# One order for GpSimd's transfers in the experts' loop, TensorE transposes for slots 1 to 3, and transposing transfers that wait for two weight quarters

## The chip, the cores and the metric

The kernel runs on one core of a Trainium2 chip. The metric is the device time of one execution in microseconds (us), taken from before the first instruction to after the last.

## The reference

Two stages follow each other. The first is attention over 8 batches, 8 heads, 576 positions and 64 channels; the heads 0 to 3 see a window of the last 32 positions, the heads 4 to 7 every 32nd position. The second sends each of the 4608 resulting rows of 512 numbers to one of 8 experts and scales the answer by the gate's probability.

```
scores = where(mask[head], q @ k.T / sqrt(64), -1e9)
x = softmax(scores) @ v                  # 8 batches x 576 rows -> 4608 x 512
logits = x @ w_gate + modality_bias[modality_id]
e = argmax(logits); gate = softmax(logits)[e]
out = gate * (relu(x @ w1[e]) @ w2[e])   # 512 -> 1024 -> 512, float32
```

## The kernel before

**Attention and routing.** Batches are taken in four pairs (1152 rows each). A pair's result is written to DRAM as `xd`, its routing is computed, and a table `ld` in DRAM gets one entry for each row: where it came from and its gate. `slots(ph)` turns the counts of each expert into a plan of slots: `li` holds the table positions of each slot's rows, `wi` the places of its weights. Of the pairs 0 to 3, the end of pair 1 brings phase 0 (slots 0 and 1), that of pair 2 phase 1 (slots 2 and 3), and that of pair 3 phase 2 (all the rest). Pair 3's last attention work and its routing overlap the first expert slots.

**The experts' loop.** A slot is 384 rows that go to one expert. There are 12 of them in a fixed loop, then one slot of 128 rows, and a guarded remainder that does not run on these inputs. `ffn` works through a slot in 8 steps f. Each step takes 1/8 of the expert's weights out of `raw`, splits them into a rounded part `wh` (ScalarE, L919) and a remainder `wl` (VectorE, L920), multiplies the rows into `h` (12 matmuls, L884), forms `hh` on ScalarE (L887) and `hl` on VectorE (L889), and two steps later adds them into three sums `o` (9 matmuls, L898). At the end ScalarE scales `o` into `y` and GpSimd scatters `y` into `out` (L906, three transfers).

**The transfers of a slot.** All are issued by GpSimd as indirect transfers, and GpSimd issues them strictly in its own row: three lookups `le` (L754, from `ld` by `li`), three gathers `fx` of the rows (L746, from `xd` by `le`), four weight quarters `raw0` to `raw3` (L763, 1 MB each, read at f = 0 and 1, 2 and 3, and so on) and three scatters `out`. Each quarter has one buffer, so the next slot's quarter waits for the last cast of the present one: quarter j of the next slot is asked for at f = 2j+1.

**Turning the rows.** TensorE needs the rows transposed. Slot 0 and the slot of 128 rows are turned by TensorE (`turn_tokens`). For the others `send_tokens` (called at f = SEND = 1 of the slot before) copies the two 16-bit halves apart on VectorE (L855) and issues three transposing transfers on SyncE's queue (L858), and `split_tokens` (at f = SPLIT = 5) puts the halves together on VectorE (L867) and splits the rows in `xh` (ScalarE, L871) and `xl` (VectorE, L872). The tile `work` of this path takes turns in the two buffers that attention's `xt` tiles use.

**What sets the order.** TensorE's row is as written during attention. Everywhere else a scheduler orders each engine's row by its own estimate of times, unless a step is pinned.

Of the kernel before, what the change touches and what calls it, by code (L numbers as in the profile page):

```python
# [11 lines left out]
F32 = mybir.dt.float32  # L12
# [30 lines left out]
LAG = 2  # L43
SEND, SPLIT = 1, 5
BIG = -float(2 ** 30)
# [135 lines left out]
def attention_moe(ctx: ExitStack, tc: tile.TileContext, a, out):  # L181
# [453 lines left out]
    def slots(ph):  # L635
# [101 lines left out]
        return li, wi, inc, wall  # L737

    def tokens(n, le, xrows):

        xt = pre.tile([P, TH, DM], F32, tag="fx", name=f"fx{n}")
        bounds = {} if xrows > NT else {"bounds_check": xrows - 1, "oob_is_err": False}
        if n.startswith("0_"):
            nc.gpsimd.memset(xt[:], 0.0)
        for h in range(TH):
            nc.gpsimd.indirect_dma_start(xt[:, h, :], None, xd[0:xrows, :], IOA(ap=le[:, h, 0:1], axis=0), **bounds)  # L746
        return xt, le

    def entries(n, li, s, xrows):

        le = pre.tile([P, TH, 2], I32, tag="le", bufs=7, name=f"le{n}")
        last = min(xrows, NT)
        for h in range(TH):
            nc.gpsimd.indirect_dma_start(le[:, h, :], None, ld[0:1 + last, :], IOA(ap=li[:, s, h:h + 1], axis=0))  # L754
        return le
# [3 lines left out]
    def weights(wi, s, j, pinned=False):  # L759

        if j not in raws:
            raws[j] = (pre if j < 2 else pools["fp"]).tile([P, 2, 1024], F32, bufs=1, name=f"raw{j}")
        ins = nc.gpsimd.indirect_dma_start(  # L763
            raws[j].rearrange("p f c -> p (f c)"), None, a["w"], IOA(ap=wi[:, s, j:j + 1], axis=0),
            bounds_check=E * 4 * P - 1, oob_is_err=False)
        if pinned:
            pin(ins)

    pools = {}

    def half_entries():
        le = pre.tile([P, TH, 2], I32, tag="le", bufs=7, name="leh")
        nc.gpsimd.indirect_dma_start(le[:, 0, :], None, ld[:], IOA(ap=halved["li"], axis=0))
        return le

    def half_tokens(le):
        xt = pre.tile([P, TH, DM], F32, tag="fx", name="fxh")
        nc.gpsimd.indirect_dma_start(xt[:, 0, :], None, xd[:], IOA(ap=le[:, 0, 0:1], axis=0))
        return xt, le
# [16 lines left out]
    def half_ffn(fp, le, xs):  # L796
# [10 lines left out]
        for f in range(8):  # L807
            raw = raws[f // 2][:, f % 2, :]
            wh = fp.tile([P, 1024], F32R, tag="wh", bufs=4, name=f"whh{f}")
            wl = fp.tile([P, 1024], F32R, tag="wl", bufs=4, name=f"wlh{f}")  # L810
            nc.scalar.copy(wh[:, 0:512], raw[:, 512:1024])
# [12 lines left out]
        settle(0)  # L824
        y = fp.tile([P, DM], F32, tag="y", bufs=2, name="yh")
        nc.scalar.mul(y[:], os[0], le[:, 0, 1:2].bitcast(F32))
        outs.add(nc.gpsimd.indirect_dma_start(
            out, IOA(ap=le[:, 0, 0:1], axis=0), y[:], None, bounds_check=NT - 1, oob_is_err=False))

# [15 lines left out]
    def halves(t):  # L845

        return t.bitcast(U16).rearrange("p a (c w) -> p a c w", w=2)

    def send_tokens(n, xt, le):

        part = TH * DM
        work = ap.tile([P, 9, DM], F32, tag="xt", bufs=2, name=f"work{n}").rearrange("p k c -> p (k c)")
        rows = work[:, 0:part].bitcast(U16).rearrange("p (h w c) -> p h w c", h=TH, w=2)
        for w in range(2):
            pin(nc.vector.tensor_copy(rows[:, :, w, :], halves(xt)[:, :, :, w]))  # L855
        cols = work[:, part:2 * part].bitcast(U16).rearrange("p (h w c q) -> p h w c q", h=TH, w=2, c=4)
# [18 lines left out]
    def ffn(fp, n, xh, xl, le, between, load=None):  # L875
# [25 lines left out]
        def finish():  # L901
            gate = le[:, :, 1].bitcast(F32)
            for h in range(TH):
                y = fp.tile([P, DM], F32, tag="y", bufs=2, name=f"y{n}{h}")
                nc.scalar.mul(y[:], os[h], gate[:, h:h + 1])  # L905
                outs.add(nc.gpsimd.indirect_dma_start(  # L906
                    out, IOA(ap=le[:, h, 0:1], axis=0), y[:], None, bounds_check=NT - 1, oob_is_err=False))

# [4 lines left out]
        for f in range(8):  # L913
            raw = raws[f // 2][:, f % 2, :]
            wh = fp.tile([P, 1024], F32R, tag="wh", bufs=4, name=f"wh{n}{f}")
            wl = fp.tile([P, 1024], F32R, tag="wl", bufs=4, name=f"wl{n}{f}")
# [4 lines left out]
            if load and f % 2:  # L921
                load(f // 2)
# [6 lines left out]
    for bp in range(NBP):  # L929
        xt = ap.tile([P, 9, DM], F32, tag="xt", bufs=2, name=f"xt{bp}")  # L930
# [33 lines left out]
    for ph, (bp, n) in enumerate(PHASES):  # L964
        last = ph == len(PHASES) - 1
        for i in range(NSTATIC - len(plan) if last else n):
            plan.append((f"{ph}_{i}", ph, i, NT + 1 if last else (bp + 1) * T2))

    def load(k, j):
        if k == len(plan):  # L970
            weights(halved["wi"], 0, j)
        if k < len(plan):
            weights(tables[plan[k][1]][1], plan[k][2], j)

# [31 lines left out]
    for n in range(nu + 3):  # L1006
# [48 lines left out]
    half_ffn(fp, *turned[len(plan)])  # L1055


# [39 lines left out]
```

## Time and profile before

| | us |
|---|---|
| runs | 632.78, 633.19, 639.26 (median 633.19) |
| profiled execution, its own time | 640.56 |
| profiled execution, span of its instructions | 638.8 |
| TensorE busy in that span | 584.8 (92%) |
| VectorE, ScalarE, GpSimd busy | 395.6, 327.4, 190.8 |

The rows further down are from the profiled execution. Their times count from the first instruction of the span. The first `hh` of a slot marks where the slot's TensorE work has begun, so the distance of two such rows is what one slot took.

### The profile page before, as it was taken

What the parts mean: (1) busy time and instruction counts of PE and PEld (TensorE: products, weight loads), DVE (VectorE), ACT (ScalarE), POOL (GpSimd) and SP (SyncE); (2) the same over time, 40 slices, a digit from 0 to 9 for tenths busy, and PEclk for the clock granted to TensorE, in tenths of its full rate; (3) what the DMA queues carried; (4) which work ended last, traced back from release to release, by engine and by line L of the source; (5) the groups of instructions that cost most, each with busy time, mean ns of one, the idle gap of its engine ahead of it and who ended that gap; (6) DMA issues with size and microseconds to landing.
All of it is one profiled execution on the core that took longest, in us unless ns stands there. A gap on an engine that the chain in (4) does not pass through costs nothing.

```text
span 638.8 us, 13548 instructions
## 1 busy us (share of the span) xinstructions
PE 584.8 (92%) x5423; PEld 512.8 (80%) x5425; DVE 395.6 (62%) x931; ACT 327.4 (51%) x650; POOL 190.8 (30%) x184
## 2 busy tenths in 40 slices
PE   8789988967996999966999999999999998999996
PEld 5677777855875989954999999898999987899985
DVE  6776867932983768913666656666666662765432
ACT  5588778634772443512545454544445542645443
POOL 3010000062244231373462626151515140212211
PEclk9899899985998999995999999999999999899999
DMA  8997988866479248447493516460505069232411
GB/s 306 278 300 249 332 234 310 272 236 204 162 264 251 92 157 180 135 98 229 149 200 146 132 67 167 180 136 2 148 1 139 11 157 156 91 73 83 166 66 70
DMA packets 63227, 105.86 MB, mean 166 GB/s; under 512 B 42099, under 2 KB 42355, under 8 KB 59060
## 3 DMA queue, kind: packets, MB, share of 16 engines
q0 software_dynamic: 14592, 52.75, 25.9%
q1 hardware_dynamic: 43284, 42.21, 25.5%
q10 hardware_dynamic: 5280, 9.94, 4.5%
q8 instruction: 45, 0.74, 0.5%
q14 instruction: 26, 0.21, 0.1%
HBM read 98.28 MB, written 19.18 MB: 184 GB/s over the span
## 4 chain that ended last, share of the span: by engine, by line
PE 68%; issue 5%; DMA 4%; DVE 3%; ACT 2%; another core or an unknown queue 1%; POOL 0%; SPq 0%; ACTq 0%; POOLq 0%; DVEq 0%
PE o L898 30%; PE h L884 30%; DMA work<-work 3%; PE s L320 1%; PE o L355 1%; DMA vv<-in_vl 1%; ACT wh L919 1%; PE ot L452 1%; PE ss L407 1%; PE xs L214 1%; PE en L597 1%; PE hh L815 0%; PE t L214 0%; PE lg L501 0%
## 5 line engine op out<-in xcount | busy, mean ns | idle before, releaser
L920 DVE TENSOR_TENSOR wl<-raw,wh 128x512 fp32r<-128x512 f32 x192 | 124.7, 688 | 36.1 <-ACT wh L919 33.2
L919 ACT CAST wh<-raw 128x512 fp32r<-128x512 f32 x192 | 109.2, 619 | 66.6 <-PE o L898 54.5
L884 PE MATMUL h<-xh,wh 128*128 128x384 f32 x384 | 130.7, 340 | 6.3 <-ACT wh L919 6.3
L884 PE MATMUL h<-xh,wl 128*128 128x384 f32 x384 | 130.6, 341 | 4.8 <-DVE wl L920 3.8
L884 PE MATMUL h<-xl,wh 128*128 128x384 f32 x384 | 130.8, 341 | 1.1 <-issue 1.1
L887 ACT ACTIVATE hh<-h 128x384 fp32r<-128x384 f32 x96 | 47.2, 492 | 155.8 <-PE h L884 110.3
L889 DVE SCALAR_TENSOR_TENSOR hl<-h,hh 128x384 fp32r<-128x384 f32 x96 | 53.4, 556 | 115.8 <-ACT hh L887 84.3
L898 PE MATMUL o<-wh,hh 128*128 128x512 f32 x288 | 115.8, 402 | 8.1 <-issue 7.2
L898 PE MATMUL o<-wl,hh 128*128 128x512 f32 x288 | 114.6, 398 | 0.1
L763 POOL DMA_INDIRECT raw<-in_w,wi x48 | 58.4, 1218 | 185.3 <-DVE wl L920 143.9
L898 PE MATMUL o<-wh,hl 128*128 128x512 f32 x288 | 110.3, 398 | 1.2 <-issue 1.2
L884 PEld LDWEIGHTS h<-xh,wh 128*128 128x128 f32 x384 | 73.2, 191 | 13.2 <-ACT wh L919 6.7
L884 PEld LDWEIGHTS h<-xh,wl 128*128 128x128 f32 x384 | 73.2, 191 | 8.3 <-DVE wl L920 4.2
L884 PEld LDWEIGHTS h<-xl,wh 128*128 128x128 f32 x384 | 73.1, 190 | 4.8 <-issue 1.2
L898 PEld LDWEIGHTS o<-wh,hh 128*128 128x128 f32 x288 | 55.2, 192 | 18.2 <-issue 8.5
L898 PEld LDWEIGHTS o<-wl,hh 128*128 128x128 f32 x288 | 55.3, 192 | 9.6 <-issue 0.4
L898 PEld LDWEIGHTS o<-wh,hl 128*128 128x128 f32 x288 | 54.8, 191 | 8.9 <-issue 1.6
L906 POOL DMA_INDIRECT out<-y,le x36 | 36.9, 1024 | 68.2 <-ACT y L905 65.2
L746 POOL DMA_INDIRECT fx<-xd,le x36 | 38.9, 1080 | 12.5 <-issue 8.6
L754 POOL DMA_INDIRECT le<-ld,li x36 | 36.2, 1006 | 17.6 <-issue 9.8
L855 DVE COPY work<-fx 128x1536 uint16<-128x1536 uint16 x22 | 37.4, 1743 | 0.0
L320 PE MATMUL s<-qk,qd 128*64 128x64 f32 x576 | 24.5, 230 | 11.3 <-issue 10.6
(191 smaller groups left out, 757.5 us busy)
## 6 DMA issues: line engine op xcount, KB each, us to landing
qk<-in_qkl SPq DMA_DIRECT2D x16, 592.0 KB
vv<-in_vl SPq DMA_DIRECT2D x16, 585.0 KB
qks<-in_qks SPq DMA_DIRECT2D x16, 576.0 KB
xd<-xt ACTq DMA_DIRECT2D x8, 1024.0 KB
vs<-in_vs SPq DMA_DIRECT2D x16, 288.0 KB
xd<-xt ACTq DMA_DIRECT2D x4, 256.0 KB
raw<-in_w,wi POOLq DMA_INDIRECT x48
le<-ld,li POOLq DMA_INDIRECT x36
```

The source lines that it names most:

```text
L320: nc.tensor.matmul(s[64 * jj:64 * jj + 64, g, :], qd[:, i, :, :].rearrange("p b q -> p (b q)"), qk[:, 18 + i:20 + i, :].rearrange("p b q - ...
L746: nc.gpsimd.indirect_dma_start(xt[:, h, :], None, xd[0:xrows, :], IOA(ap=le[:, h, 0:1], axis=0), **bounds)
L754: nc.gpsimd.indirect_dma_start(le[:, h, :], None, ld[0:1 + last, :], IOA(ap=li[:, s, h:h + 1], axis=0))
L763: ins = nc.gpsimd.indirect_dma_start(raws[j].rearrange("p f c -> p (f c)"), None, a["w"], IOA(ap=wi[:, s, j:j + 1], axis=0), bounds_check= ...
L855: pin(nc.vector.tensor_copy(rows[:, :, w, :], halves(xt)[:, :, :, w]))
L884: nc.tensor.matmul(hp, w[:, a1], x[:, c, :], start=(k == 0), stop=(k == 11))
L887: nc.scalar.activation(hh[:], hp, AF.Relu)
L889: nc.vector.scalar_tensor_tensor(hl[:], hp, 0.0, hh.bitcast(F32), ALU.max, ALU.subtract)
L898: nc.tensor.matmul(os[h], hx[:, m], w[:, 512:1024], start=(f == 0 and i == 0), stop=(f == 7 and i == 2))
L906: outs.add(nc.gpsimd.indirect_dma_start(out, IOA(ap=le[:, h, 0:1], axis=0), y[:], None, bounds_check=NT - 1, oob_is_err=False))
L919: nc.scalar.copy(wh[:, c], raw[:, c])
L920: nc.vector.tensor_tensor(wl[:, c], raw[:, c], wh[:, c].bitcast(F32), ALU.subtract)
```

## The change

The edits, in the order of the code:

1. `in_turn` ties every GpSimd transfer of the experts' loop to the one before it in program order, so the scheduler no longer chooses their order. Inside a slot the written order is now: quarter 0, the three scatters of the slot before, quarter 1, lookups (f = 3, three slots ahead), gathers (f = 4, two slots ahead), quarters 2 and 3.
2. `raw2` and `raw3` lie in the buffer of attention's tile `xt0` instead of the pool that opens when attention ends, and slot 0's two are asked for right behind slot 0's turning. `work` then has only the other buffer, `xt1`.
3. Slots 1 to 3 are turned by TensorE at f = 4 of the slot before (`TURN`, `TURNED`).
4. For slots 4 to 11 the two copies L855 stay at f = 1 (`PLANE`), the transposing transfers are issued at f = 3 (`SEND`) and wait until quarter 1 of that step has landed; the next slot's first gather waits until they have landed; `split_tokens` moves from f = 5 to f = 6.
5. `wh` and `wl` have 5 buffers instead of 4, `y` 4 instead of 2, `le` 5 instead of 7. The slot of 128 rows is turned at f = 4 instead of 3.

```diff
-SEND, SPLIT = 1, 5
+PLANE, SEND, SPLIT, TURN = 1, 3, 6, 4
+FIND, GATHER = 3, 4
+WHEN = {1: 0, 3: 1, 5: 2, 7: 3}
+TURNED = 4
...
+    def in_turn(ins):
+        if ordered:
+            if ordered[-1]:
+                tc.add_manual_dep(ins.ins, ordered[-1], behind, reason="order of transfers")
+            ordered.append(ins.ins.name)
+        return ins
...
         for h in range(TH):
-            nc.gpsimd.indirect_dma_start(xt[:, h, :], None, xd[0:xrows, :], IOA(ap=le[:, h, 0:1], axis=0), **bounds)
+            ins = in_turn(nc.gpsimd.indirect_dma_start(
+                xt[:, h, :], None, xd[0:xrows, :], IOA(ap=le[:, h, 0:1], axis=0), **bounds))
+            if h == 0:
+                for t in turning:
+                    after_landing(ins, t)
...
-            raws[j] = (pre if j < 2 else pools["fp"]).tile([P, 2, 1024], F32, bufs=1, name=f"raw{j}")
+            if j < 2:
+                raws[j] = pre.tile([P, 2, 1024], F32, bufs=1, name=f"raw{j}")
+            else:
+                both = ap.tile([P, 9, DM], F32, tag="xt0", name="raw23")[:, 0:8, :]
+                both = both.rearrange("p (j f a) c -> p j f (a c)", j=2, f=2)
+                raws[2], raws[3] = both[:, 0], both[:, 1]
...
-        work = ap.tile([P, 9, DM], F32, tag="xt", bufs=2, name=f"work{n}").rearrange("p k c -> p (k c)")
+        work = ap.tile([P, 9, DM], F32, tag="xt1", name=f"work{n}").rearrange("p k c -> p (k c)")
...
+        turning.clear()
         for h in range(TH):
-            nc.sync.dma_start(
+            turning.append(nc.sync.dma_start(
                 cols[:, h].rearrange("p w c q -> p (w c) q"),
-                rows[:, h].rearrange("p w (c q) -> p (w c) q", q=P), transpose=True)
+                rows[:, h].rearrange("p w (c q) -> p (w c) q", q=P), transpose=True))
+            after_landing(turning[h], quarter[1])
...
         if n == nu + 1:
             turn(0)
+            for j in (2, 3):
+                load(0, j)
...
-    for j in (2, 3):
-        load(0, j)
+    ordered.append(None)
     for k, (n, *_) in enumerate(plan):
         def between(f):
             pop(POPF)
-            if k + 1 < len(plan):
+            if TURNED <= k + 1 < len(plan):
+                if f == PLANE:
+                    sent[k + 1] = plane_tokens(plan[k + 1][0], *gathered[k + 1])
                 if f == SEND:
-                    sent[k + 1] = send_tokens(plan[k + 1][0], *gathered[k + 1])
+                    sent[k + 1] = send_tokens(*sent[k + 1])
                 if f == SPLIT:
                     turned[k + 1] = split_tokens(plan[k + 1][0], (k + 1) % 2, *sent[k + 1])
-            elif f == 3:
+            elif f == TURN:
                 turn(k + 1)
-            if f == 2:
+            if k == 0 and f == 0:
+                look_up(2)
+            if f == FIND:
+                look_up(k + 3)
+            if f == GATHER:
                 gather(k + 2)
-            if f == 4:
-                look_up(k + 3)
```

In the rows of instructions below, the number behind a name tells instances apart; `le_0`, `fx_1` and the like count the slots inside a phase, so `le_0_4041` before and `le_0_4004` after are the lookups of slot 4, the first slot of phase 2.

**GpSimd where slot 0 runs.** Before, from the last two quarters of slot 0 on:

```order
L763 DMA raw_3344<-in_w,wi_2389 128x2048
L763 DMA raw_2515<-in_w,wi_2389 128x2048
L763 DMA raw_2519<-in_w,wi_2389 128x2048
L754 DMA le_0_3519<-ld,li_3216 128x2 x3
L754 DMA le_1_3603<-ld,li_3216 128x2 x3
L746 DMA fx_0_3523<-xd,le_0_3519 128x512 x3
L746 DMA fx_1_3961<-xd,le_1_3603 128x512 x3
L763 DMA raw_3340<-in_w,wi_2389 128x2048
```

After, the same stretch:

```order
L771 DMA le_0_3408<-ld,li_3216 128x2 x3
L786 DMA raw_2515<-in_w,wi_2389 128x2048
L786 DMA raw_2519<-in_w,wi_2389 128x2048
L771 DMA le_1_3554<-ld,li_3216 128x2 x3
L759 DMA fx_0_3616<-xd,le_0_3408 128x512 x3
L786 DMA raw_3294<-in_w,wi_2389 128x2048 x2
```

The lookups of slots 2 and 3 stood together and directly ahead of both slots' gathers; now two weight quarters stand between them, and slot 3's gathers have moved to a later slot.

**GpSimd where slots 1 and 2 run.** Before, all twelve lookups of slots 4 to 7 follow each other as soon as `li` of phase 2 is there:

```order
L754 DMA le_0_4041<-ld,li_3860 128x2 x3
L754 DMA le_1_4349<-ld,li_3860 128x2 x3
L754 DMA le_2_4657<-ld,li_3860 128x2 x3
L754 DMA le_3_4965<-ld,li_3860 128x2 x3
L906 DMA out<-y_10_4237,le_1_2399 4608x512
L906 DMA out<-y_11_4242,le_1_2399 4608x512
L746 DMA fx_0_4275<-xd,le_0_4041 128x512 x3
L746 DMA fx_1_4583<-xd,le_1_4349 128x512
L763 DMA raw_2519<-in_w,wi_3225 128x2048
L746 DMA fx_1_4583<-xd,le_1_4349 128x512 x2
L763 DMA raw_3340<-in_w,wi_3225 128x2048
```

After:

```order
L786 DMA raw_2519<-in_w,wi_3225 128x2048
L771 DMA le_0_4004<-ld,li_3871 128x2 x3
L759 DMA fx_1_4066<-xd,le_1_3554 128x512 x3
L786 DMA raw_3294<-in_w,wi_3225 128x2048 x2
L786 DMA raw_2515<-in_w,wi_3225 128x2048
L938 DMA out<-y_10_4254,le_1_2399 4608x512
L938 DMA out<-y_11_4259,le_1_2399 4608x512
L938 DMA out<-y_12_4264,le_1_2399 4608x512
L786 DMA raw_2519<-in_w,wi_3225 128x2048
L771 DMA le_1_4330<-ld,li_3871 128x2 x3
L759 DMA fx_0_4392<-xd,le_0_4004 128x512 x3
```

The lookups of slots 4 to 7 are spread over four slots, three at a time, each set between two weight quarters.

**GpSimd in a later slot.** Before, the gathers and lookups stand ahead of quarter 1, and nothing in this row waits for a transposing transfer:

```order
L763 DMA raw_2515<-in_w,wi_3871 128x2048
L906 DMA out<-y_00_5161,le_0_4041 4608x512
L906 DMA out<-y_01_5166,le_0_4041 4608x512
L906 DMA out<-y_02_5171,le_0_4041 4608x512
L746 DMA fx_4_5507<-xd,le_4_5273 128x512 x3
L754 DMA le_7_6197<-ld,li_3860 128x2 x3
L763 DMA raw_2519<-in_w,wi_3871 128x2048
L763 DMA raw_3340<-in_w,wi_3871 128x2048
```

After:

```order
L786 DMA raw_2515<-in_w,wi_3882 128x2048
L938 DMA out<-y_40_6425,le_4_5272 4608x512
L938 DMA out<-y_41_6430,le_4_5272 4608x512
L938 DMA out<-y_42_6435,le_4_5272 4608x512
L786 DMA raw_2519<-in_w,wi_3882 128x2048
L799 DMA leh<-ld,li_3871 128x2
L759 DMA fx_7_6538<-xd,le_7_6196 128x512 x3
L786 DMA raw_3294<-in_w,wi_3882 128x2048 x2
```

Quarter 1 stands ahead of the lookups and gathers, and the first gather, with quarters 2 and 3 (`raw_3294` holds both) behind it, waits for the landing of transfers that themselves wait for quarter 1.

## Rows read from the trace of the kernel before

**Rows 1.** The page: busy time of each engine, share of the span, instructions.

```profile
PE 584.8 (92%) x5423; PEld 512.8 (80%) x5425; DVE 395.6 (62%) x931; ACT 327.4 (51%) x650; POOL 190.8 (30%) x184
```

**Rows 2.** Timeline, ScalarE, first `hh` of slots 0 to 4, 9, 10: start, duration.

```profile
183.35 0.53 ACT L887 ACTIVATE hh<-h 128x384 fp32r<-128x384 f32 x1
...
227.59 0.49 ACT L887 ACTIVATE hh<-h 128x384 fp32r<-128x384 f32 x1 [3.25 <-PE h L884]
...
263.13 0.49 ACT L887 ACTIVATE hh<-h 128x384 fp32r<-128x384 f32 x1 [0.68 <-PE h L884]
...
311.96 0.49 ACT L887 ACTIVATE hh<-h 128x384 fp32r<-128x384 f32 x1 [1.73 <-PE h L884]
...
345.34 0.49 ACT L887 ACTIVATE hh<-h 128x384 fp32r<-128x384 f32 x1 [1.94 <-PE h L884]
...
512.47 0.49 ACT L887 ACTIVATE hh<-h 128x384 fp32r<-128x384 f32 x1 [1.94 <-PE h L884]
...
551.46 0.49 ACT L887 ACTIVATE hh<-h 128x384 fp32r<-128x384 f32 x1 [1.99 <-PE h L884]
```

**Rows 3.** Windows: stretch, its length, busy time of PE, PEld, DVE, ACT, POOL, clock, DMA.

```profile
139.00:151.00 12.00, 3.68 (x29) 2.60 (x30) 0.00 (x0) 1.19 (x3) 7.70 (x8) 0.63 0.52 147
...
198.50:204.80 6.30, 0.05 (x1) 0.00 (x0) 0.35 (x3) 0.66 (x2) 2.48 (x3) 0.90 1.01 271
...
281.00:298.00 17.00, 5.73 (x12) 3.02 (x11) 0.56 (x1) 0.74 (x2) 10.19 (x11) 0.63 0.67 204
...
312.00:512.40 200.40, 200.40 (x1009) 181.71 (x1008) 128.21 (x180) 98.33 (x174) 83.71 (x74) 1.00 0.42 113
```

**Rows 4.** Timeline, GpSimd, 133 to 149: first and last of 12 transfers.

```profile
133.75 0.96 POOL L754 DMA_INDIRECT le<-ld,li  x1 [2.88 <-DVE li L711]
...
147.97 1.00 POOL L746 DMA_INDIRECT fx<-xd,le  x1 [0.30 <-issue]
```

**Rows 5.** Timeline, GpSimd, 186 to 202: first and last of 12 transfers.

```profile
186.49 0.97 POOL L754 DMA_INDIRECT le<-ld,li  x1 [1.56 <-DVE li L711]
...
200.86 1.00 POOL L746 DMA_INDIRECT fx<-xd,le  x1 [0.30 <-issue]
```

**Rows 6.** Timeline, GpSimd, 266 to 294: first and last of 22 transfers.

```profile
266.26 0.98 POOL L754 DMA_INDIRECT le<-ld,li  x1 [3.08 <-DVE li L711]
...
293.23 1.01 POOL L763 DMA_INDIRECT raw<-in_w,wi  x1 [0.30 <-issue]
```

**Rows 7.** Timeline, TensorE, 283 to 292: the longest gap.

```profile
283.68 0.34 PE L884 MATMUL h<-xh,wl 128*128 128x384 f32 x1 [1.06 <-issue]
291.23 0.80 PE L898 MATMUL o<-wh,hh 128*128 128x512 f32 x1 [7.21 <-issue]
```

**Rows 8.** Timeline, GpSimd, 320 to 334: first and last of 9 transfers.

```profile
320.82 1.34 POOL L906 DMA_INDIRECT out<-y,le  x1 [1.71 <-ACT y L905]
...
332.19 1.01 POOL L763 DMA_INDIRECT raw<-in_w,wi  x1 [0.30 <-issue]
```

**Rows 9.** Chain of waits, 515 to 546, slot 9.

```profile
523.72 17.47 DMA work<-work
```

**Rows 10.** Chain of waits, 170 to 184: slot 0 turned by TensorE.

```profile
173.76 1.46 PE xt L214 x12
```

**Rows 11.** Timelines, slot 8: transposing transfers, quarter 1, first copy of `split_tokens`.

```profile
487.63 4.52 SPq L858 DMA_TRANSPOSE work<-work  x3
...
494.09 1.00 POOL L763 DMA_INDIRECT raw<-in_w,wi  x1 [0.31 <-issue]
...
499.96 2.00 DVE L867 COPY work<-work 128x1536 uint16<-128x1536 uint16 x2
```

**Rows 12.** DMA, 487 to 497, 40 slices of 0.25 us: GB/s.

```profile
GB/s 0 0 0 229 426 393 0 128 220 218 200 198 116 133 115 115 131 421 263 254 276 304 350 164 344 306 277 145 182 152 325 382 312 295 36 1 0 0 0 0
```

**Rows 13.** DMA, 209 to 217, 40 slices of 0.2 us: GB/s, one quarter alone.

```profile
GB/s 0 0 0 0 0 0 0 0 0 41 410 287 0 0 82 492 451 369 451 451 410 451 451 369 410 123 0 0 0 0 0 0 0 0 0 0 0 0 0 0
```

**Rows 14.** Timeline, GpSimd: the issue of that quarter.

```profile
209.30 1.00 POOL L763 DMA_INDIRECT raw<-in_w,wi  x1 [7.44 <-DVE wl L920]
```

More of the change, by code (lines that the diff above doesn't have):

```diff
@@ L737, in slots @@
         return li, wi, inc, wall
+    ordered = []
+    behind = mybir.DependencyInfo(mybir.DependencyClass.NoSync, mybir.DependencyReason.DATA)
+    def in_turn(ins):
[4 more added lines that the diff above has]
+        return ins
     def tokens(n, le, xrows):
@@ L745, in tokens @@
         for h in range(TH):
-            nc.gpsimd.indirect_dma_start(xt[:, h, :], None, xd[0:xrows, :], IOA(ap=le[:, h, 0:1], axis=0), **bounds)
+            ins = in_turn(nc.gpsimd.indirect_dma_start(
[3 more added lines that the diff above has]
+                    after_landing(ins, t)
         return xt, le
     def entries(n, li, s, xrows):
-        le = pre.tile([P, TH, 2], I32, tag="le", bufs=7, name=f"le{n}")
+        le = pre.tile([P, TH, 2], I32, tag="le", bufs=5, name=f"le{n}")
         last = min(xrows, NT)
         for h in range(TH):
-            nc.gpsimd.indirect_dma_start(le[:, h, :], None, ld[0:1 + last, :], IOA(ap=li[:, s, h:h + 1], axis=0))
+            in_turn(nc.gpsimd.indirect_dma_start(
+                le[:, h, :], None, ld[0:1 + last, :], IOA(ap=li[:, s, h:h + 1], axis=0)))
         return le
@@ L767, in weights @@
             pin(ins)
+        else:
+            in_turn(ins)
+        return ins
     pools = {}
     def half_entries():
-        le = pre.tile([P, TH, 2], I32, tag="le", bufs=7, name="leh")
-        nc.gpsimd.indirect_dma_start(le[:, 0, :], None, ld[:], IOA(ap=halved["li"], axis=0))
+        le = pre.tile([P, TH, 2], I32, tag="le", bufs=5, name="leh")
+        in_turn(nc.gpsimd.indirect_dma_start(le[:, 0, :], None, ld[:], IOA(ap=halved["li"], axis=0)))
         return le
@@ L808, in half_ffn @@
             raw = raws[f // 2][:, f % 2, :]
[L809 to L810 removed]
+            wh = fp.tile([P, 1024], F32R, tag="wh", bufs=5, name=f"whh{f}")
+            wl = fp.tile([P, 1024], F32R, tag="wl", bufs=5, name=f"wlh{f}")
             nc.scalar.copy(wh[:, 0:512], raw[:, 512:1024])
@@ L824, in half_ffn @@
         settle(0)
-        y = fp.tile([P, DM], F32, tag="y", bufs=2, name="yh")
+        y = fp.tile([P, DM], F32, tag="y", bufs=4, name="yh")
         nc.scalar.mul(y[:], os[0], le[:, 0, 1:2].bitcast(F32))
-        outs.add(nc.gpsimd.indirect_dma_start(
-            out, IOA(ap=le[:, 0, 0:1], axis=0), y[:], None, bounds_check=NT - 1, oob_is_err=False))
+        outs.add(in_turn(nc.gpsimd.indirect_dma_start(
+            out, IOA(ap=le[:, 0, 0:1], axis=0), y[:], None, bounds_check=NT - 1, oob_is_err=False)))
     def parts_of(n, odd):
@@ L855, in send_tokens @@
             pin(nc.vector.tensor_copy(rows[:, :, w, :], halves(xt)[:, :, :, w]))
+        return work, rows, le
+    def send_tokens(work, rows, le):
+        part = TH * DM
         cols = work[:, part:2 * part].bitcast(U16).rearrange("p (h w c q) -> p h w c q", h=TH, w=2, c=4)
+        turning.clear()
         for h in range(TH):
-            nc.sync.dma_start(
+            turning.append(nc.sync.dma_start(
                 cols[:, h].rearrange("p w c q -> p (w c) q"),
-                rows[:, h].rearrange("p w (c q) -> p (w c) q", q=P), transpose=True)
+                rows[:, h].rearrange("p w (c q) -> p (w c) q", q=P), transpose=True))
+            after_landing(turning[h], quarter[1])
         return work, cols, le
@@ L903, in finish @@
             for h in range(TH):
-                y = fp.tile([P, DM], F32, tag="y", bufs=2, name=f"y{n}{h}")
+                y = fp.tile([P, DM], F32, tag="y", bufs=4, name=f"y{n}{h}")
                 nc.scalar.mul(y[:], os[h], gate[:, h:h + 1])
-                outs.add(nc.gpsimd.indirect_dma_start(
-                    out, IOA(ap=le[:, h, 0:1], axis=0), y[:], None, bounds_check=NT - 1, oob_is_err=False))
+                outs.add(in_turn(nc.gpsimd.indirect_dma_start(
+                    out, IOA(ap=le[:, h, 0:1], axis=0), y[:], None, bounds_check=NT - 1, oob_is_err=False)))
         def down_last(*args):
@@ L914, in ffn @@
             raw = raws[f // 2][:, f % 2, :]
-            wh = fp.tile([P, 1024], F32R, tag="wh", bufs=4, name=f"wh{n}{f}")
-            wl = fp.tile([P, 1024], F32R, tag="wl", bufs=4, name=f"wl{n}{f}")
+            wh = fp.tile([P, 1024], F32R, tag="wh", bufs=5, name=f"wh{n}{f}")
+            wl = fp.tile([P, 1024], F32R, tag="wl", bufs=5, name=f"wl{n}{f}")
             for c0 in range(0, 1024, 512):
@@ L920, in ffn @@
                 nc.vector.tensor_tensor(wl[:, c], raw[:, c], wh[:, c].bitcast(F32), ALU.subtract)
-            if load and f % 2:
-                load(f // 2)
+            if load and f in WHEN:
+                load(WHEN[f])
             late.append(partial(down_last if f == 7 else down, f, wh, wl, *up(f, wh, wl)))
@@ L967, in attention_moe, with after_landing @@
             plan.append((f"{ph}_{i}", ph, i, NT + 1 if last else (bp + 1) * T2))
+    landed = mybir.DependencyInfo(mybir.DependencyClass.Sync, mybir.DependencyReason.DATA)
+    quarter, turning = {}, []
+    def after_landing(ins, other):
+        tc.add_manual_dep(ins.ins, other.ins.name, landed, reason="transfers kept apart")
     def load(k, j):
         if k == len(plan):
-            weights(halved["wi"], 0, j)
+            quarter[j] = weights(halved["wi"], 0, j)
         if k < len(plan):
-            weights(tables[plan[k][1]][1], plan[k][2], j)
+            quarter[j] = weights(tables[plan[k][1]][1], plan[k][2], j)
     found, gathered, sent, turned = {}, {}, {}, {}
```

8 lines of the change are left out of this document (5 added, 3 removed).

## The prediction

> **What bounds the kernel now.** I read the page's busy times first: TensorE is busy for 584.8 of 638.8 us and no other engine for more than 62% [rows 1]. A change that only lightens VectorE, ScalarE or GpSimd therefore gains nothing unless TensorE waits for them somewhere. The next view is the first `hh` of each slot, because the distance of two of them is a slot's price. From slot 4 to slot 9 that is (512.47 - 345.34) / 5 = 33.43 us, and the window from 312.0 to 512.4 shows TensorE busy for 200.40 of 200.40 us: a plain slot is pure TensorE work [rows 2, 3]. Against 33.43, slot 0 took 44.2, slot 1 35.5, slot 2 48.8 and slot 9 39.0 us [rows 2]. So 28.3 us are lost in slots 0 to 2 and 5.6 in slot 9. In the first three, part of the loss is pair 3's attention work, which TensorE does there; that work stays.
>
> Where the rest went is seen in the windows. In 281 to 298 TensorE was busy for 5.73 of 17.00 us and in 198.5 to 204.8 for 0.05 of 6.30 [rows 3]. In both stretches VectorE and ScalarE were nearly idle too, and one gap of TensorE, 7.21 us long, names no engine that it waited for [rows 7]. What did go on was GpSimd's row: from 266.26 to 294.2 it issued 22 transfers without a pause, twelve lookups first, and from 186.49 to 201.9 twelve, six lookups and six gathers [rows 5, 6]. A third run of the same sort, six lookups and six gathers from 133.75 on, again has TensorE at 3.68 busy us of 12.00 in 139 to 151 [rows 3, 4]. The counterexample is the run of nine from 320.82 to 333.2 with three lookups in it: it lies in the window without any idle TensorE time [rows 3, 8]. So three of three runs of twelve or more stop all engines, and a run of nine doesn't. The trace doesn't say by which mechanism. I call this stop the freeze.
>
> **The change part by part.**
>
> *Lookups spread out (edit 1).* The twelve lookups of slots 4 to 7 in one run become four sets of three, each with quarter 1 ahead and gathers behind. The longest run then is a set of lookups, a set of gathers and the quarters, eight or fewer where quarter 3 has to wait for its cast. By the counterexample that is below what freezes. The whole excess of slot 2 is 48.83 - 33.43 = 15.4 us [rows 2], and little of pair 3's work is left in that slot, so I take **-15.4**. Its bounds are -11.3 (the idle part of 281 to 298 alone, 17.00 - 5.73 [rows 3]) and -15.4.
>
> *The run in slot 0.* Six lookups and six gathers become three lookups, two quarters that wait for slot 0's casts, then three lookups, three gathers and two quarters. The idle time of TensorE there is 6.30 - 0.05 = 6.25 us [rows 3]. The second run can be as long as eight, close to the nine that did no harm but at a time when other transfers are many. I take half, **-3.1**, with bounds 0 and -6.25. The run at 133.75 belongs to attention, its order is unchanged, and I count nothing for it.
>
> *Slots 1 to 3 turned by TensorE (edit 3).* Slot 0's turning shows the price: 12 transposes in 1.46 us [rows 10]. TensorE has no slack in a plain slot, so all of it is added: 3 x 1.46 = **+4.4**. What it takes away, the copies L855 and L867 and the transposing transfers of those slots, lies on VectorE and on the queue and is worth nothing by itself. The Trainium skill, "TensorE: Matmul & The Clock Gate", section "Part 4: PE-mode transpose", measures about 275 ns for one 128x128 transpose in one kernel; 36 of them would be 9.9 us by that price, and the row here, at 0.12 us each, makes it less than half.
>
> *Waits for landing (edit 4).* Queued behind a transposing transfer on SyncE is only the next of its kind. Behind the waiting gather on GpSimd stand two more gathers and quarters 2 and 3, and for quarter 2 the next slot's step 4 waits, over half a slot later. VectorE waits for the transposes themselves in `split_tokens`. When do they come? Quarter 1 was issued at 494.09 in slot 8 [rows 11]. One quarter alone, issued at 209.30, moved its last bytes in the 26th slice of 0.2 us, at 214.2: 4.9 us [rows 13, 14]. So it lands at 499.0. Issue of three transposing transfers took 4.52 us, and issue to the end of traffic beside three gathers, 487.63 to about 495.8, took 8.2 [rows 11, 12]; without the gathers I take about 5, near the lower end, so they land at about 504. VectorE asks at f = 6, one step of 33.43 / 8 = 4.18 later than the 499.96 of before, at 504.1 [rows 2, 11]. It just fits: cost **0**, from 0 to 3 us in a slot (at 8.2 they land at 507.2).
>
> In slot 9 the transposing transfers stood in the chain for 17.47 us [rows 9] and cost the excess of 5.6. Waiting for quarter 1 and holding the gathers takes away just such a meeting: **-5.6**, bounds 0 and -5.6.
>
> *The rest.* Quarters 2 and 3 of slot 0 come about 20 us earlier, into attention, where nothing on TensorE waits for transfers: 0. The additional buffers give looser waits for casts and scatters: 0, since TensorE is the limit in plain slots [rows 3].
>
> *Sum.* Against the profiled execution: 640.56 - 15.4 - 3.1 - 5.6 + 4.4 = 620.9. That execution is 7.4 above the median of 633.19. I take slot 9's 5.6 to be most of that difference, so it isn't subtracted a second time from the median: 633.19 - 15.4 - 3.1 + 4.4 = 619.1, and the first way, less the remaining 1.8 between profile and median, gives 619.1 too. I predict **619**.
>
> **The rivals.**
>
> *A: the freeze isn't the run's doing.* It could belong to the stage, for instance to the end of the attention's routing, and stay wherever GpSimd's row goes. For it: the trace names no mechanism. Against: it came in three places, each in a run of twelve or more. Then only the turning is left: 633.2 + 4.4 = 637.6, no change by the 1% that a measurement of this kernel can tell (627 to 639.5).
>
> *B: the turned rows come late, and it gets slower.* The place is `split_tokens` in slots 3 to 10. Quarter 1, the transposes and the gathers now go one behind the other, and the transposes have about 5.1 us between 499.0 and 504.1, plus about 1 us before the next slot starts. From about 6 us on every further microsecond is TensorE's loss, in each slot whose quarter 1 really moves (where two slots in a row use one expert, the indices in `wi` point out of bounds and the transfer is empty). At the 17.47 of slot 9 that is 11 us, in four to eight slots 44 to 88, and the time is 619 + 44 = 663 or more. At 8.2 it is 2 us in four to eight slots, 627 to 635. For it: a price of 17.47 stands in the trace [rows 9]. Against: that one stood beside other transfers, which the waits now hold back. The Trainium skill, "DMA: Bandwidth & Descriptors", section "Rules for kernel authors", speaks for B: issue a transfer early and wait for it late, where this change issues it late. No row tells yet which price holds with the waits in place.
>
> *C: the freeze shrinks or moves.* Lookups, gathers and quarters of phase 2 still crowd into the end of slot 1 when `li` is late. If a stop of 6 to 8 us remains there, as in slot 0 before [rows 3], and slot 0's stays too, the time is 619.1 + 3.1 + 7 = 629.
>
> *D: it also frees slot 0 wholly*, 619.1 - 3.1 = 616; with a plain slot 2 and less of pair 3's overlap to pay, 612.
>
> **How the numbers follow.** The forecast with D, 612 to 624: 0.63. C and the milder price of B, 624 to 635: 0.18, half of it below 627. A: 0.10. The heavy case of B, above 640: 0.09. The range of 8 in 10 runs from 610 to 634. Faster by over 1% (below 627): 0.63 + 0.09 = 0.72. Within 1%: 0.09 + 0.10 = 0.19. Slower: 0.09.
>
> **What the profile after would show.** If I am right: slot 2 takes about 35 us instead of 48.8, slots 1 and 2 show no stretch in which all engines stop, and three sets of 12 transposes add about 1.5 us each in slots 0 to 2. Slots 4 to 11 stay at 33.4 each, and TensorE there still waits for nothing. If B holds, VectorE's copy of the turned rows waits for the transposing transfers in most slots, and TensorE for `xl` at each slot's start. If A holds, a stop of 10 us or more stands near 270 to 300 although no run of GpSimd is longer than nine. I would be wrong above all if the run's length isn't what decides, or if a late transpose costs a plain slot its full occupation.

## The result and the profile after

| | before | after |
|---|---|---|
| runs, us | 632.78, 633.19, 635.28, 639.26 | 611.66, 612.94, 616.02, 620.36 |
| median, us | 634.24 | 614.48 |
| profiled execution, us | 640.56 | 611.66 |

The ratio of after to before is 0.969, with an interval of 0.959 to 0.978. Ratios, here and below, are estimated from the undisturbed executions alone and so can differ a little from the quotient of the medians, which are those of all runs. The forecast was 619, in a range from 610 to 634. The profiled execution of before is the longest of its kind and that of after the shortest, so the two traces differ by 28.9 us where the medians differ by 19.8.

The page's first part, busy time of each engine, answers to [rows 1]:

```profile
PE 577.3 (95%) x5461; PEld 509.3 (84%) x5461; DVE 382.7 (63%) x925; ACT 328.3 (54%) x656; POOL 191.9 (31%) x184
```

The timeline of ScalarE, first `hh` of slots 0 to 3, 9 and 10, answers to [rows 2]:

```profile
178.18 0.54 ACT L919 ACTIVATE hh<-h 128x384 fp32r<-128x384 f32 x1
...
216.75 0.49 ACT L919 ACTIVATE hh<-h 128x384 fp32r<-128x384 f32 x1 [0.97 <-PE h L916]
...
253.02 0.49 ACT L919 ACTIVATE hh<-h 128x384 fp32r<-128x384 f32 x1 [1.11 <-PE h L916]
...
287.62 0.49 ACT L919 ACTIVATE hh<-h 128x384 fp32r<-128x384 f32 x1 [0.96 <-PE h L916]
...
490.87 0.49 ACT L919 ACTIVATE hh<-h 128x384 fp32r<-128x384 f32 x1 [1.54 <-PE h L916]
...
524.30 0.49 ACT L919 ACTIVATE hh<-h 128x384 fp32r<-128x384 f32 x1 [1.54 <-PE h L916]
```

Slot 2 took 34.6 us where it took 48.8, slot 9 took 33.4 where it took 39.0, slot 0 took 38.6 where it took 44.2. Slot 1 took 36.3, 0.7 more than before. And slot 0 began 5.2 us earlier, which no term of the sum said. From slot 4 on the first `hh` comes 2.6 us later within its slot than in slots 0 to 3, so slot 3 reads as 36.1 us although TensorE has no idle time in it.

Windows of after, columns as in [rows 3]:

```profile
139.00:151.00 12.00, 10.14 (x131) 8.96 (x132) 3.91 (x13) 7.01 (x16) 6.00 (x6) 0.50 0.77 248
186.00:200.00 14.00, 12.01 (x62) 10.02 (x62) 5.21 (x21) 2.36 (x8) 9.37 (x10) 0.96 0.88 316
253.00:288.00 35.00, 35.00 (x183) 31.82 (x182) 16.66 (x28) 16.92 (x32) 13.70 (x13) 1.00 0.67 236
318.00:552.00 234.00, 234.00 (x1178) 212.30 (x1177) 149.83 (x211) 114.45 (x203) 94.88 (x85) 1.00 0.39 112
```

Slot 2 (253 to 288) and all plain slots are pure TensorE work. Two stops are left, smaller: in 139 to 151 TensorE was busy for 10.14 us instead of 3.68, and in slot 0 it lost 2.0 us. GpSimd's timeline of after shows what stood there; the number in brackets is the pause before a transfer:

```profile
136.85 0.95 POOL L771 DMA_INDIRECT le<-ld,li  x1 [0.30 <-issue]
140.32 1.01 POOL L759 DMA_INDIRECT fx<-xd,le  x1 [2.52 <-DMA le<-ld,li]
...
182.77 1.01 POOL L771 DMA_INDIRECT le<-ld,li  x1 [17.96 <-DVE li L714]
...
197.11 1.00 POOL L786 DMA_INDIRECT raw<-in_w,wi  x1 [0.30 <-issue]
```

From 182.77 to 198.1 there are again twelve transfers without a pause. Around 140 the twelve of [rows 4] were broken in two, since the gathers this time waited 2.52 us for the lookups' landing, in a part of the kernel that the change doesn't touch. Slot 2 holds a run too, of eleven (three scatters, quarter 1, three lookups, three gathers, quarter 2), longer than the nine at most that the prediction expected, and TensorE has no idle time there. Its first and last transfer:

```profile
258.73 1.02 POOL L938 DMA_INDIRECT out<-y,le  x1 [5.75 <-ACT y L937]
...
272.49 1.00 POOL L786 DMA_INDIRECT raw<-in_w,wi  x1 [0.30 <-issue]
```

In the plain slots the wait for transposing transfers has moved to GpSimd. The waits of 318 to 560 have none of VectorE for them, and this one (us in total, times, longest):

```profile
POOL fx L759 <- DMA work<-work: 37.0, 6, 10.0
```

### The profile page after: what moved, and what is told of

Read it like the earlier page. It is cut to its first block, busy times and chain, and to the rows that moved or that the text cites. A ratio compares the mean times of both kernels' runs of the same rounds, so it can differ in the third digit from the quotient of the medians.

```text
span 609.9 us, 13599 instructions
## 1 busy us (share of the span) xinstructions
PE 577.3 (95%) x5461; PEld 509.3 (84%) x5461; DVE 382.7 (63%) x925; ACT 328.3 (54%) x656; POOL 191.9 (31%) x184
## 4 chain that ended last, share of the span: by engine, by line
PE 76%; issue 3%; ACT 1%; DVE 1%; POOL 0%; ACTq 0%; POOLq 0%
PE o L930 33%; PE h L916 33%; PE s L323 1%; PE ss L410 1%; PE o L358 1%; PE ot L455 1%; PE xs L217 1%; PE lg L504 1%; ACT wh L951 1%; PE xt L217 1%; PE ts L217 1%; PE en L600 1%; PE t L217 1%; PE hh L841 0%; PE xl L217 0%
## 5 line engine op out<-in xcount | busy, mean ns | idle before, releaser
L916 PE MATMUL h<-xl,wh 128*128 128x384 f32 x384 | 129.0, 336 | 0.0
L916 PE MATMUL h<-xh,wh 128*128 128x384 f32 x384 | 128.1, 337 | 0.0
L930 PE MATMUL o<-wh,hl 128*128 128x512 f32 x288 | 114.3, 397 | 0.7 <-issue 0.7
L930 PE MATMUL o<-wh,hh 128*128 128x512 f32 x288 | 113.4, 394 | 1.0 <-issue 1.0
L786 POOL DMA_INDIRECT raw<-in_w,wi x48 | 60.7, 1264 | 70.4 <-DVE wl L952 38.6
L759 POOL DMA_INDIRECT fx<-xd,le x36 | 36.8, 1022 | 55.7 <-DMA work<-work 44.6
L594 POOL TENSOR_TENSOR hv<-hb,val 128x576 f32<-128x576 bf16 x4 | 5.1, 1282 | 83.6 <-DVE hb L585 46.1
```

The costliest lines, as they stand in the source:

```text
L759: ins = in_turn(nc.gpsimd.indirect_dma_start(xt[:, h, :], None, xd[0:xrows, :], IOA(ap=le[:, h, 0:1], axis=0), **bounds))
L786: ins = nc.gpsimd.indirect_dma_start(raws[j].rearrange("p f c -> p (f c)"), None, a["w"], IOA(ap=wi[:, s, j:j + 1], axis=0), bounds_check= ...
L916: nc.tensor.matmul(hp, w[:, a1], x[:, c, :], start=(k == 0), stop=(k == 11))
L930: nc.tensor.matmul(os[h], hx[:, m], w[:, 512:1024], start=(f == 0 and i == 0), stop=(f == 7 and i == 2))
```

## The experiments

Ratios are to the kernel before on the same chip. The experiments fell on four chips, and on three of them the kernel before took 605 to 608 us, not 634; these three are called calm below. That turned out to be the main finding, so each entry names the time of before beside it.

**Order alone.** The kernel before with `in_turn` around the loop's GpSimd transfers, nothing else:

```diff
-            nc.gpsimd.indirect_dma_start(le[:, h, :], None, ld[0:1 + last, :], IOA(ap=li[:, s, h:h + 1], axis=0))
+            in_turn(nc.gpsimd.indirect_dma_start(le[:, h, :], None, ld[0:1 + last, :], IOA(ap=li[:, s, h:h + 1], axis=0)))
...
+    ordered.append(None)
     for k, (n, *_) in enumerate(plan):
```

> The kernel before with the first edit alone: the transfers of the loop in program order, nothing else changed. Run theory (a long unbroken run of GpSimd transfers stops the engines): the twelve lookups in a row are gone, slot 2 falls from 48.8 to about 34 us, and the whole from 634 to 617 to 622. Stage theory (the stop belongs to the end of attention's routing and stays wherever GpSimd's row goes): a stretch of 10 us or more without TensorE work remains between slot 1 and slot 3, and the time stays at 630 to 638.

608.3 us, before 606.2, ratio 1.002 (0.997 to 1.007). Neither theory foresaw a chip without the loss. No general stop is seen, with or without the twelve lookups in a row. Instead, slot 0 lost 4.7 us to a late transposing transfer. The chain of 190 to 212:

```profile
187.94 16.63 DMA work<-work
```

And TensorE's waits there:

```profile
PE h L896 <- DVE wl L932: 4.7, 1, 4.7
```

**Slots 1 to 3 by transposing transfers again.**

```diff
-TURNED = 4
+TURNED = 1
```

> The changed kernel with slots 1 to 3 turned by transposing transfers again (TURNED = 1). If the three turnings on TensorE cost 3 x 1.46 us on the path and give nothing back: 614.5 - 4.4 = 610. Rival, the turning is what keeps transposing transfers out of the crowded slots 0 to 2: VectorE waits there for them, a slot of the first three gets 3 us or more longer, and the time is 614 to 622.

606.2, before 606.2, ratio 1.004 (0.999 to 1.010). The changed kernel itself is at 0.988 and 0.995 on two other chips of this kind (below), so no gain from giving up the three turnings is seen. TensorE was busy for 40.88 of 45 us in 245 to 290, and one of its waits there is for a turned slot:

```profile
PE h L916 <- ACT xh L903: 2.6, 1, 2.6
```

The rival's wait is there: this profile loses 4.1 us in that stretch, about what the three turnings cost. Whether the turnings win anything on balance isn't shown, since the changed kernel itself wasn't timed on this chip.

**No waits for landing.**

```diff
-            if h == 0:
-                for t in turning:
-                    after_landing(ins, t)
...
-            after_landing(turning[h], quarter[1])
```

> The changed kernel without the two waits for landing: transposing transfers go at f = 3 at once, and the next gathers don't wait for them. If the waits keep transfers from meeting and that is worth something: VectorE's copy of the turned rows waits for transposing transfers in some of the slots 4 to 11, with 3 to 6 us lost in each such slot, 617 to 630. If they are worth nothing: 614.5 within 3 us, every plain slot at 33.4.

606.1, before 606.2, ratio 1.002 (0.998 to 1.006); TensorE was busy for 230.00 of 230 us from 318 to 548. In this profile no plain slot needs the waits. As before, the changed kernel wasn't timed beside it, so what the waits cost or give here is not measured.

**A long run in a plain slot.** The changed kernel with nine more lookups, into tiles that nothing reads:

```diff
             if f == FIND:
                 look_up(k + 3)
+                if k == 6:
+                    for r in range(3):
+                        spare(r, plan[k + 1])
```

> The changed kernel with nine more lookups (into spare tiles that nothing reads) behind the three at f = 3 of slot 6, so that GpSimd issues quarter 1, twelve lookups, three gathers and quarter 2 without a pause in a plain slot, far from any routing. Run theory: TensorE stops for about 8 us or more before the run's end and slot 6 takes 40 us or more instead of 33.4. Stage theory: slot 6 takes 33.4. Fetch theory (the stop needs a fetch of one of TensorE's instruction blocks, queue 8 of the page, inside the run): such a fetch falls into this run too, so also 40 or more.

604.1, before 606.2. GpSimd's timeline, first and last of 22 transfers without a pause, 30 us:

```profile
385.52 1.02 POOL L945 DMA_INDIRECT out<-y,le  x1 [8.12 <-ACT y L944]
...
414.89 1.01 POOL L793 DMA_INDIRECT raw<-in_w,wi  x1 [0.30 <-issue]
```

The window around it:

```profile
380.00:420.00 40.00, 40.00 (x204) 36.51 (x204) 25.40 (x36) 20.20 (x37) 25.00 (x23) 1.00 0.28 70
```

The DMA view's line on queue 8, which the fetch theory takes for TensorE's instruction blocks, in 386 to 416:

```profile
q8 instruction: 1, 0.02, 0.3%
```

A run as long as the longest of those that had stopped all engines (22, the other two had 12) cost nothing here, with an instruction block in it. So on this chip neither the length of a run nor a fetch inside it does harm. What either would do where the kernel before takes 634 this single execution can't say.

**The kernel before, unchanged, and the changed one, unchanged**, on one other chip.

> The kernel before, unchanged, for a second profile. The chip that ran the first experiments gave it a median of 606 us where the chip of the comparison gave 634. Run theory: its twelve lookups in a row stop the engines here as well, slot 2 takes about 48 us. Chip theory (the stop needs something that only some chips or hours have, and the long runs are only where it shows): where the time is near 606, no stretch of 5 us or more without TensorE work lies between 130 and 300 us, and slot 2 takes 34 to 36 us; where it is near 634, the stops are back.

> The changed kernel, unchanged, beside the kernel before on one chip. Chip theory: where the kernel before takes about 606, the changed one has no stop to remove, pays 4.4 us for the turnings on TensorE, wins some of it back in slots 0 to 2, and comes out at 603 to 611, within 1% of before; where before takes about 634, the changed one is 15 to 24 us faster. Run theory: 15 to 20 us faster than before on any chip.

Before 605.2 and 605.5, after 603.4, ratio 0.988 (0.981 to 0.995): the chip theory's numbers, except that the ratio lies a little beyond its 1%. The windows of before show no stop in slot 0, and one loss of 6.4 us between 270 and 290:

```profile
171.00:205.00 34.00, 34.00 (x189) 29.80 (x188) 23.40 (x56) 15.18 (x30) 17.64 (x16) 1.00 0.84 247
...
270.00:290.00 20.00, 13.60 (x67) 11.56 (x65) 7.65 (x10) 4.43 (x8) 9.82 (x10) 0.95 1.09 299
```

That loss has a cause that the trace names. In the timeline, GpSimd's first of the twelve lookups, the first scatter behind them and a later lookup, and ScalarE's last `y` of slot 2:

```profile
241.97 0.97 POOL L754 DMA_INDIRECT le<-ld,li  x1 [3.29 <-DVE li L711]
...
257.02 1.18 POOL L906 DMA_INDIRECT out<-y,le  x1 [0.30 <-DMA le<-ld,li]
...
280.77 0.98 POOL L754 DMA_INDIRECT le<-ld,li  x1 [5.08 <-DMA out<-y,le]
...
290.01 0.69 ACT L905 ACTIVATE y<-o,le 128x512 f32<-128x512 f32 x1 [8.19 <-DMA out<-y,le]
```

TensorE's waits of 240 to 330:

```profile
PE o L898 <- ACT hh L887: 7.5, 1, 7.5
```

Slot 1's scatters stand behind the twelve lookups on GpSimd, and the last of them, issued at 271.87, took 8.15 us to land. GpSimd's next three lookups waited for that landing, and slot 2's scatters stood behind them. With two buffers, slot 2's last `y` waits for the first of those scatters to land, `hh` stands behind that `y` on ScalarE, and TensorE waits 7.5 us. The changed kernel has no idle TensorE time from 178 to 330. But it began its slots 6.0 us later (first `hh` at 175.0 instead of 169.0), and 2.6 us of that is TensorE's wait for `hv`. The chains of after, then of before, at that place (start, us, what):

```profile
156.40 0.35 POOL raw L786
...
157.69 0.99 POOL raw L786
158.71 1.17 POOL hv L594
159.93 2.13 PE en L600 x18
```

```profile
155.35 1.15 PE ot L452 x32
156.50 1.15 PE en L597 x18
```

Slot 0's quarters 2 and 3, moved up by the change, stand ahead of the product `hv` on GpSimd, and the first of them waits for attention's work (ScalarE's `et` stands ahead of it in the chain). TensorE's `en`, which makes the entry table, waits for `hv`.

**After once more, `y` alone, and the quarters behind `hv`**, together on a third chip.

> The changed kernel once more, with more rounds and beside the next two. Chip theory: where the kernel before takes about 606, the changed one takes 601 to 607, up to 1% faster; where before takes about 634, it takes 611 to 620. Run theory: 15 us or more faster on any chip.

> The kernel before with one part of the change alone: y has four buffers instead of two. The twelve lookups in a row stay. Scatter theory (where no general stop is seen, the long run costs time through the scatters queued behind it: ScalarE's third y waits for a scatter to land, hh stands behind that y, and TensorE waits 7.5 us for it, as in the second profile of before): the wait of y for a scatter goes, slot 2 and 3 lose 7 us less, and the time falls from 605.5 to 598 to 600. Rival, the wait only moves to the next transfer in the queue (gathers of the next slot, weight quarters): 603 to 607.

> The changed kernel, with slot 0's quarters 2 and 3 tied behind GpSimd's product hv of pair 2's routing, which they stood ahead of. Queue theory (quarter 2 waits there for the end of pair 2's use of xt0, hv and with it the entry table wait behind it, and slot 0 begins some 4 us later): slot 0 begins 3 to 5 us earlier and the time falls by 2 to 5 us against the changed kernel on the same chip. Rival, hv is not on the path: no difference.

```diff
-                y = fp.tile([P, DM], F32, tag="y", bufs=2, name=f"y{n}{h}")
+                y = fp.tile([P, DM], F32, tag="y", bufs=4, name=f"y{n}{h}")
```

```diff
             for j in (2, 3):
                 load(0, j)
+                tc.add_manual_dep(quarter[j].ins, hvs[-1].ins.name, behind, reason="behind hv")
```

Before 607.9. After: 603.7, ratio 0.995 (0.990 to 0.999). Before with four `y`: 602.8, ratio 0.992 (0.987 to 0.998). The quarters behind `hv`: 597.3, ratio 0.986 (0.981 to 0.992), 6.4 below the changed kernel, the best of all on this kind of chip. In the two profiles slot 0 begins 2.5 us earlier (166.7 instead of 169.2) and the spans differ by 2.3, so the expected cause shows for that much; the rest of the 6.4 isn't located. GpSimd's timeline of that one has `hv` first:

```profile
150.84 1.15 POOL L596 TENSOR_TENSOR hv<-hb,val 128x576 f32<-128x576 bf16 x1 [4.20 <-DVE hb L587]
152.15 1.04 POOL L788 DMA_INDIRECT raw<-in_w,wi  x1 [0.15 <-issue]
```

With four `y` the wait for the scatter is gone, 250 to 290 is all TensorE work, but the profile (an execution of 604.8 us, where the fastest took 594.7) lost as much one slot later, where SyncE and the transfers took 21 us to turn a slot's rows beside the gathers, lookups and weights. The window, the chain, and TensorE's wait:

```profile
290.00:312.00 22.00, 15.78 (x70) 14.02 (x69) 9.46 (x14) 6.74 (x12) 7.02 (x6) 0.84 0.88 129
```

```profile
283.60 7.50 SPq L858
...
291.15 13.40 DMA work<-work
```

```profile
PE h L884 <- DVE wl L920: 6.2, 1, 6.2
```

So the scatter theory holds for its wait. For the time its forecast amounts to a ratio of 0.988 to 0.991 and the rival's to 0.996 to 1.002; 0.992 lies between them, and the interval doesn't decide.

**The waits for landing again, and early sending**, both on the version with the quarters behind `hv`. These three fell on a chip where the kernel before takes 634.1.

> The version with slot 0's quarters 2 and 3 behind hv once more, as the base for the next two and to see whether its gain returns on another chip. Queue theory: 596 to 602 where before takes about 606, that is 1% or more faster than before. Rival, the earlier 597 was that chip's luck: 602 to 606.

> The same, without the two waits for landing (transposing transfers at f = 3 at once, gathers not held). If the waits are worth something: one slot in some executions loses 3 to 6 us to a late transposing transfer, the median rises by 2 to 5 us against the base, and the runs spread more. If they are worth nothing with the transfers in one order: the median stays within 2 us.

> The same without the waits and with the transposing transfers sent at f = 1 and used at f = 5, as in the kernel before. If sending early and using late is what counts: no wait for transposing transfers anywhere, within 2 us of the base. If meeting the scatters, quarter 0 and the gathers is what makes them late: VectorE waits for them in one or more slots, and the median is 3 to 10 us above the base.

The edit of the second is that of the run without waits above; the third has besides:

```diff
-PLANE, SEND, SPLIT, TURN = 1, 3, 6, 4
+PLANE, SEND, SPLIT, TURN = 1, 1, 5, 4
```

With the waits: 618.1, ratio 0.976 (0.970 to 0.981). Without: 627.4, ratio 0.987 (0.981 to 0.993). Sent early: 634.3, ratio 1.002 (0.998 to 1.005). When the transposing transfers go and what waits for them decides, on this kind of chip, whether a gain is left in the total. The gain in slot 2 doesn't hang on it: in all three profiles slot 2 takes 33.8 us. First `hh` of slots 2 and 3 where the transfers are sent early:

```profile
262.17 0.49 ACT L919 ACTIVATE hh<-h 128x384 fp32r<-128x384 f32 x1 [1.91 <-PE h L916]
...
295.97 0.49 ACT L919 ACTIVATE hh<-h 128x384 fp32r<-128x384 f32 x1 [0.96 <-PE h L916]
```

What that run loses, it loses mainly in slots 4 to 8 (34.1 to 35.1 us instead of 33.4) and in slot 9 (41.4). The base's forecast of 596 to 602 was for the calm kind; on this kind its 0.976 beside the changed kernel's 0.969 shows no gain from the tie to `hv`.

Windows of 330 to 530, with the waits, then without:

```profile
330.00:530.00 200.00, 200.00 (x1007) 181.53 (x1006) 127.67 (x181) 97.95 (x174) 84.44 (x76) 1.00 0.40 112
```

```profile
330.00:530.00 200.00, 197.44 (x989) 178.04 (x988) 121.25 (x172) 93.87 (x169) 79.50 (x75) 1.00 0.46 103
```

18 matmuls fewer in the same time: the plain slots are no longer pure TensorE work. Slots 4 to 8 take 33.7 to 34.7 us, 3.9 more in sum than with the waits. Slot 4 shows how. First with the waits, GpSimd's last lookup and first gather, and ScalarE's `hh` of the step:

```profile
343.78 0.94 POOL L773 DMA_INDIRECT le<-ld,li  x1 [0.30 <-issue]
349.14 0.94 POOL L761 DMA_INDIRECT fx<-xd,le  x1 [4.42 <-DMA work<-work]
...
347.08 0.48 ACT L921 ACTIVATE hh<-h 128x384 fp32r<-128x384 f32 x1
```

Then without: first and last of GpSimd's run, ScalarE's cast and `hh`, the last matmul of that `h`:

```profile
336.50 1.02 POOL L938 DMA_INDIRECT out<-y,le  x1 [7.20 <-ACT y L937]
...
349.31 1.00 POOL L787 DMA_INDIRECT raw<-in_w,wi  x1 [0.30 <-issue]
...
348.94 1.14 ACT L951 CAST wh<-raw 128x512 fp32r<-128x512 f32 x2 [5.23 <-remote]
352.55 0.49 ACT L919 ACTIVATE hh<-h 128x384 fp32r<-128x384 f32 x1 [2.47 <-PE h L916]
...
347.03 0.33 PE L916 MATMUL h<-xh,wl 128*128 128x384 f32 x1
```

From the scatters to quarter 2 GpSimd issues eleven transfers without a pause, and meanwhile ScalarE seems not to learn what TensorE has done: `hh` starts 5.5 us after the start of the last matmul of its `h`, and the cast ahead of it waited 5.23 us for a release from an unnamed source. The same delay of about 5 us stands in each of slots 3 to 8. With the waits in place the run is cut after seven by a pause of 4.42 us, and `hh` starts 0.6 us after the start of that matmul.

The length of the run alone doesn't explain it. In slot 2 of the same execution the same eleven go without a pause and delay nothing; the difference that the trace shows is that the first transposing transfer of the kernel goes in slot 3, at 305.76. The waits change both at once, the run's length and what goes beside the transposing transfers, and no run parts the two.

Slot 9 adds 3.1 us (36.5 instead of 33.4) in the run without waits, of which TensorE waited 2.6 for late turned rows: the transposing transfers took 20.37 us in the chain. Where the transfers are sent early, TensorE's wait there is longer, as [rows 9] had it:

```profile
DVE work L899 <- DMA work<-work: 11.9, 1, 11.9
...
PE h L916 <- ACT xh L903: 5.4, 1, 5.4
```

## Why the prediction was right, and where it wasn't

**The freeze and its bound.** The forecast rested on the reading that long unbroken runs of GpSimd transfers stop all engines [rows 4 to 6]. That fits in part where the kernel before takes 634: slots 0 and 2 stopped before, the twelve left in slot 0 still stop, and in the later runs eleven in a row delay ScalarE by 5 us in slots 3 to 8. But eleven in slot 2 cost nothing there, and twelve in slot 0 cost 2.0 us where they had cost 6.25, so the length isn't all of it there either; the prediction's own runs of nine at most didn't come about, and its gain came all the same. It doesn't hold where before takes 606: 22 transfers in a row cost nothing there. No full stop was seen without such a run, but a run isn't enough for one, and the reading, drawn from one chip, was taken for a property of the kernel. That the comparison fell on the kind of chip that the profile of before came from was luck for the forecast: on the calm kind the same change gave 0.5 to 1.2%. The two kinds of chip differ by 28 us for the kernel before, 11 for the changed one and 21 for the version with the quarters behind `hv`. What they differ in, no run here tells, and as each chip was met once, chip and hour can't be told apart. The long runs of the experts' loop aren't all of it: of the 25 us between the two profiles of the version with the quarters behind `hv`, 19 have arisen before slot 0 begins (185.6 against 166.7).

**The terms.** Slot 2: forecast -15.4, measured 34.6 - 48.8 = -14.2 with the 1.4 to 1.5 us of a turning in it, so -15.7. Slot 0's run: forecast -3.1 with bounds 0 and -6.25, measured 38.6 - 44.2 = -5.6 with a turning, so about -7, beyond the bound. And not for the reason given: the quarters between the lookups did not wait for casts, the run stayed twelve long, and the stop shrank all the same. Why it shrank isn't shown; the transposing transfers that stood beside it before had gone with the turning on TensorE. Slot 9: -5.6, as said. Turning: slot 1 got 0.7 longer where 1.5 were counted. In sum -24.7 from the slots, against -19.7 (15.4 + 3.1 + 5.6 - 4.4) in the forecast for the profiled pair.

**What was counted at nothing.** The run at 133.75 was left out because its order is unchanged. In the profile of after it stopped TensorE for about 1.9 us of 12 instead of 8.3, and slot 0 began 5.2 us earlier. The order didn't change but a pause came in; whether the change brought it or the execution, one profile can't say, and in a later profile on the same kind of chip (the version with the quarters behind `hv`) the stop there was long again, 3.6 busy us in the 12 from 140 to 152, though that part of the code is the same.

The move of quarters 2 and 3 was priced at 0 with the words that nothing on TensorE waits for transfers there. That was the wrong queue: the cost is on GpSimd's own row, where `hv` stood behind them. The row of the kernel after shows it, and I hadn't followed that engine past the moved step. On the calm kind of chip it cost the changed kernel 6.4 us by the medians, of which the profiles show 2.3 to 2.5. In the profile of the comparison `hv` waited 4.29 us for VectorE anyway, so nothing showed in the result.

**The waits for landing** were taken at 0 to 3 us a slot with the gain in slot 9 alone. Their cost was 0, as the plain slots show. Their worth was mis-sized: 9.3 us by the medians (627.4 - 618.1) where before takes 634, against 5.6 in the sum. The two profiles differ by 7.1, 3.9 of it in slots 4 to 8, where `hh` comes late, and 3.1 in slot 9, the meeting that the term was meant for. On the calm kind the run without them had TensorE busy throughout the plain slots. Rival B, the late turned rows, didn't come: no VectorE wait for transposing transfers is left in the plain slots of after. The Trainium skill, "DMA: Bandwidth & Descriptors", section "Rules for kernel authors", advises to issue a transfer early and wait for it late. Here issuing early didn't pay: sent at f = 1 and used at f = 5, the kernel took 634.3 us, against 627.4 sent at f = 3 and used at f = 6, both without waits for landing, and 618.1 with them. That the early transfers met others fits the profile's slot 9, where the turned rows came late; the loss in the other slots isn't traced that far.

**Rival A** (the stop belongs to the stage) is refuted on that kind of chip by slot 2, in the comparison and in the three later profiles, and **C** came true in a small form: 2 us of the stop in slot 0 remained. Which edit took the stop out of slot 2 isn't parted: the twelve lookups in a row and the transposing transfers left it together (the first one now goes at 303.16, in slot 3), and the order alone was run on a calm chip only.

Why signals between engines come late on some chips while GpSimd issues stays open, and so does what the transposing transfers have to do with it. How the stop grows with the run's length wasn't tried either: the long run in a plain slot fell on a calm chip.

## What to carry to other kernels

A stop that names no releaser may be the chip's and not the kernel's: time the kernel before on a second chip before building on it. Try GpSimd's transfers in sets of a few, with a wait between them that something needs anyway: no plain slot of these kernels lost time to that, and on the chip where signals came late it was worth 9 us. When a step moves up, read each engine's row behind its new place, since a step that waits there holds up whatever stood next, as `hv` did.

## What the runs showed of the hardware

- The same program took 605 to 608 us on three chips and 634 on one or two others, each met once, with medians that agree within 0.5% inside each kind.
- On the slower kind, ScalarE's `hh` began 5.5 us after the start of the last matmul that it needs while GpSimd issued eleven indirect transfers in a row and transposing transfers went beside them, 0.6 us after it where the eleven were cut by a pause. On the other kind, 22 in a row left TensorE busy for 40.00 of 40 us.
- A set of three transposing transfers took 13.40 us, 16.63 us, 17.47 us [rows 9] and 20.37 us in the chains where it came late, and TensorE waited 2.6 to 6.2 us each time.
